# Turning half of the normalised rows by transposing transfers, in a kernel of two attention and two state-space layers

## The chip, the cores and the metric

The kernel runs on one core of one Trainium2 chip. The metric is the device time of one execution in microseconds, the median over several runs. A core has TensorE (matmuls, PE in the profile; its weight loads are PEld), ScalarE (ACT), VectorE (DVE), GpSimd (POOL), SyncE (SP, which here only issues transfers) and 16 DMA engines that serve the transfers of all queues. SBUF is the working memory of 128 partitions, PSUM the accumulators that TensorE writes.

## The reference

Four layers over a sequence of 2048 rows of 640 channels; each adds to its input what it computes from the normalised input. Layers 1 and 3 are attention with 32 heads of 20 channels, layers 2 and 4 a state-space convolution over the whole sequence (through an FFT):

```python
def _layernorm(x, axis=-1, eps=1e-5):
    m = jnp.mean(x, axis=axis, keepdims=True)
    v = jnp.var(x, axis=axis, keepdims=True)
    return (x - m) / jnp.sqrt(v + eps)

qkv = (x @ wqkv).reshape(B, S, 3, H, Dh).transpose(2, 0, 3, 1, 4)
p = softmax(einsum("bhqd,bhkd->bhqk", q, k) * Dh ** -0.5)
o = einsum("bhqk,bhkd->bhqd", p, v).transpose(0, 2, 1, 3).reshape(B, S, D) @ wo

K = 2.0 * einsum("dn,dnl->dl", C, exp(A * dt * pos)).real     # the filter of the convolution
y = irfft(rfft(u_t, 2 * L) * rfft(K, 2 * L))[:, :, :L] + u * D_skip

x = x + attention(layernorm(x)); x = x + s4d(layernorm(x))
x = x + attention(layernorm(x)); x = x + s4d(layernorm(x))
```

## The kernel before

The kernel is one program for a tile framework: the Python code issues instructions in an order, and a scheduler then places them on each engine. It goes by the order written as a priority and lets an instruction go first whose inputs are there earlier. On the chip every engine, and every engine's queue of transfers, then works through its own list strictly in order.

`attention` (from line 432) runs twice, once for layer 1 (`first_layer`) and once for layer 3. It has two parts. The long second part computes scores, exponentials and values wave by wave; ScalarE's exponentials fill it. This document is about the short first part (from line 756), the front, which makes what the first waves need:

- The 2048 rows are taken as 16 tiles of 128 rows, in four sets of four (`i4` = 0 to 3). In the first layer `load_x` loads a set from memory, into two buffers for each of the four tiles, so that one set can be loaded while another is worked on. In the later layer the rows lie in SBUF already.
- `ln_stats` gives mean and 1/deviation of each row (VectorE, with one square root on ScalarE). ScalarE then writes the normalised rows, f32, four activations of 128 x 640 a set (in the trace `xr<-xr,nb,rs` in the first layer and `xn<-x,nb,rs` in the later one).
- The projections need the rows turned, channels on the partitions. TensorE turns them in 128 x 128 blocks (line 823, tile `pst`): for each of five groups of channels (`ct`) four transposes fill one PSUM tile of 128 x 512. Each value is held as a sum of two f16 parts: ScalarE casts the PSUM tile into `xh` and VectorE writes the difference into `xl`. `xh` and `xl` are 128 x 5 x 2048 and hold all turned rows.
- `block0(i4)` (line 767) projects the set onto the first 128 columns of q and of k: for each 15 matmuls of 512 columns, five channel groups by three products of parts (`pq`, line 773). ScalarE copies the result (`qc`), and `post` (line 510) squares it, splits it into f16 parts `qhi` and `qlo` (two buffers each) and sends them to memory (`qs`, `ks`) by the SP queue.
- `values4(i4)` (line 779) computes v for the four tiles, 15 matmuls each (`pv`, line 586): 480 columns in the first layer, 160 in the later one. VectorE and ScalarE copy the result into `V`.
- The loop runs stats, normalisation, turning, `block0(i4)` and then `values4(i4 - 1)`, so the values lag a set behind. After the loop follow the norms of q and k (`norms`, `nrm`), their maximum (`longest`), the shift that goes to memory and comes back (`shift`, `qm`, `qop`), the first loads of `kop` and `qop`, and `values4(3)`.
- The scores' PSUM tiles are made from the space that the front's four `S` and two `M` tiles leave.

In the first layer a generator (`kgen`, line 198) makes powers for the convolution's filter beside all this: VectorE reduces angles, ScalarE takes exponentials and sines (`ke_`, `ks_`, `kc_`), SP stores them to memory (`wd`). The scheduler weaves its instructions into the front.

The two selectors that `norms` needs are loaded as f32 into a tile of their own (`self_`) and copied to `sel` at the first set.

Of the kernel before, what the change touches and what calls it, by code (L numbers as in the profile page):

```python
# [21 lines left out]
P = 128  # L22
L = 2048
D = 640
NI = L // P
NCT = D // P
H = 32
# [7 lines left out]
NBLK = len(BLOCKS)  # L35
# [11 lines left out]
QW = DH * 8  # L47
# [40 lines left out]
def mha_s4d_kernel(ctx, tc, x_in, wqkv, wo, lar, aim, cr, ci, ldt, dsk,  # L88
# [12 lines left out]
    se, ve, ge, sy = (Ordered(e, plan, tie, e is nc.vector) for e in (nc.scalar, nc.vector, nc.gpsimd, nc.sync))  # L101
# [330 lines left out]
    def attention(x, stats):  # L432
# [50 lines left out]
        def stage(c0, n, tag, dst=None, pool=None):  # L483

            full = QW if pool or tag == "v" else P
            ts = tag + "s" if pool else "ws"
            wt = (pool or q2).tile([P, NCT, QW], F32, tag=ts, bufs=1, name=ts)[:, :, :n]
            cols = c0 if isinstance(c0, tuple) else (c0,)
            m = n // len(cols)
            for k, c_ in enumerate(cols):  # L490
                sy.dma_start(wt[:, :, k * m:k * m + m], wqkv[:, c_:c_ + m].rearrange("(t p) c -> p t c", p=P))

            def make():
                bufs = 1 if tag == "v" else 2
# [12 lines left out]
            return make  # L507
# [249 lines left out]
        with ExitStack() as c2:  # L757
            psum(c2, M=2, S=4)
            hp = c2.enter_context(tc.tile_pool(name="hp", bufs=1))
            xp = c2.enter_context(tc.tile_pool(name="xnp", bufs=2))  # L760
            self_ = hp.tile([P, NBLK * H], F32, name="self")
            NQ = 3 if first_layer else 1
            wv = [hp.tile([P, NCT, NQ * QW], F16, name=f"wv{n}") for n in range(2)]
            wb = [[hp.tile([P, NCT, P], F16, name=f"wb{w_}{n}") for n in range(2)] for w_ in range(2)]
# [14 lines left out]
            def values4(i4):  # L779
                for i in range(4 * i4, 4 * i4 + 4):  # L780
                    for _ in values_of(i, 0, pst("M", [P, 512], F32, tag="mm", name="pv"), wv, NQ * QW):
                        pass

            def load_x(i4):

                if x is not None:
                    return [x[:, 4 * i4 + i, :] for i in range(4)]
                ts = [xp.tile([P, D], F32, tag=f"xr{i}", name=f"xr{i}") for i in range(4)]
                for i, t in enumerate(ts):
                    sy.dma_start(t, xv[:, 4 * i4 + i, :])  # L790
                return ts
# [4 lines left out]
                filler[:2] = kgen(), False  # L796
                weave(1)
            sy.dma_start(self_, c_sel)
            for i4 in range(4):
                xr = coming  # L800
                if i4 < 3:
                    coming = load_x(i4 + 1)
                if stats is None:
                    mv, rs = ln_stats(lambda i: xr[i], 4)
                else:
                    mv, rs = stats(i4)
                xn = []
                nb = sm.tile([P, 4], F32, tag="nb", name="nb")
                ve.scalar_tensor_tensor(nb, mv[:, :, 0], -1.0, rs, ALU.mult, ALU.mult)
                for i in range(4):  # L810
                    t = xr[i] if x is None else xp.tile([P, D], F32, tag=f"xr{i}", name=f"xn{i}")
                    se.activation(t, xr[i], AF.Identity, scale=rs[:, i:i + 1], bias=nb[:, i:i + 1])
                    xn.append(t)
                if i4 == 0:
                    for make in made_:
                        make()
                    made_ = [stage(2 * D + q * QW, QW, f"b{q}", [w[:, :, q * QW:q * QW + QW] for w in wv], hp)
                             for q in range(NQ)]
                    ve.tensor_copy(sel, self_)
                for ct in range(NCT):  # L820
                    pt = pst("S", [P, 512], F32, tag="S", name="pst")
                    for i in range(4):
                        te.transpose(pt[:, i * P:i * P + P], xn[i][:, ct * P:ct * P + P], ident)
# [3 lines left out]
                block0(i4)  # L827
                if i4 == 0:
                    for make in made_:
                        make()  # L830
                    nxt.append(stage((P, D + P), 64, "w"))
                else:
                    values4(i4 - 1)
# [960 lines left out]
```

## Time and profile before

| | |
|---|---|
| median of 3 runs | 2646.85 us (2645.38 to 2647.79) |
| profiled execution: span from first to last instruction | 2647.0 us |
| front of the first layer, first transpose to first scores | 17.5 to 115.8 us of the span |
| front of the later layer, first transpose to first scores | 1404.9 to 1468.6 us |
| granted TensorE clock, mean | 0.994 |

The profiled execution's own time is its span; it differs from the median of the runs by 0.15 us, so times taken from its trace can be set against the median as they stand. Times inside the trace are microseconds from the start of the span. Line 78 is a helper through which most instructions of VectorE, ScalarE, POOL and SP are issued, so these are told apart by their tiles, not by their line. TensorE's matmuls are pipelined: the start of the next one, not the length of one, says how much of the engine it took.

### The profile page before, as it was taken

How to read it: one execution, taken by the hardware profiler on the slowest of the kernel's cores; microseconds unless marked ns; L12 is line 12 of the kernel's file. 1: busy time of each engine (PE TensorE's matmuls, PEld its weight loads, DVE VectorE, ACT ScalarE, POOL GpSimd, SP SyncE). 2: the span in 40 equal slices, each digit the busy share in tenths (PEclk: the TensorE clock that was granted, in tenths of full speed). 3: DMA queues.
4: the chain of work that ended last, by engine and by line, in shares of the span. 5: the costliest groups of instructions: out<-in, count | busy, mean ns of one | idle time of the engine just before them, and what ended most of it. 6: DMA issues, size and time to landing. Idle time of an engine off the chain costs nothing.

```text
span 2647.0 us, 118800 instructions
## 1 busy us (share of the span) xinstructions
PE 2492.4 (94%) x52388; PEld 1409.8 (53%) x52388; DVE 1519.5 (57%) x3430; ACT 2344.0 (89%) x2763; POOL 801.7 (30%) x1230
## 2 busy tenths in 40 slices
PE   6899999999999999899898999999999998999898
PEld 3444444454444444587896544454444443444898
DVE  7587777777765887577786323232232222143875
ACT  7899999999999999655665899999999999999574
POOL 1123333233323332111681122222222223222285
PEclk9999999999999999999999999999999999999999
DMA  6522222322222221654652111121121113222466
GB/s 206 189 53 77 68 74 62 82 65 63 61 54 59 53 63 38 234 206 163 213 173 64 47 53 50 51 60 45 45 66 39 50 34 87 71 66 61 137 190 184
DMA packets 188158, 241.99 MB, mean 91 GB/s; under 512 B 43504, under 2 KB 128816, under 8 KB 186224
## 3 DMA queue, kind: packets, MB, share of 16 engines
q1 hardware_dynamic: 151936, 188.28, 22.6%
q0 software_dynamic: 35696, 46.01, 7.4%
q8 instruction: 413, 6.77, 1.1%
q14 instruction: 113, 0.93, 0.1%
HBM read 158.16 MB, written 76.00 MB: 88 GB/s over the span
## 4 chain that ended last, share of the span: by engine, by line
ACT 59%; PE 20%; issue 10%; DVE 3%; DMA 2%; POOL 1%; SPq 0%; ACTq 0%; POOLq 0%; DVEq 0%
ACT pt L78 57%; PE psy L1430 3%; PE pa L903 2%; PE psv L1430 2%; PE po L193 2%; PE psx L1430 2%; PE S L868 2%; PE pst L1452 1%; PE pkx L193 1%; PE pv L586 1%; PE m L620 1%; PE pkt L196 1%; PE pq L773 1%; DMA kb<-khb 1%; DMA kop<-ks 1%
## 5 line engine op out<-in xcount | busy, mean ns | idle before, releaser
L78 ACT ACTIVATE pt<-S 128x1024 f32<-128x1024 f32 x2048 | 1927.7, 1033 | 27.9 <-PE S L868 15.5
L903 PE MATMUL pa<-pt,V 64*32 64x512 f32 x16384 | 1096.9, 589 | 1.4 <-DVE oc L78 1.4
L868 PE MATMUL S<-qop,kop 61*32 61x512 f16 x16384 | 877.2, 380 | 82.7 <-ACT pt L78 67.8
L868 PEld LDWEIGHTS <-kop 61*32 61x32 f16 x16384 | 366.9, 89 | 737.3 <-issue 619.2
L903 PEld LDWEIGHTS pa<-pt,V 64*32 64x32 f32 x16384 | 312.7, 106 | 72.0 <-issue 8.6
L78 POOL DMA_DIRECT2D dn<-oc x248 | 122.7, 501 | 574.2 <-DVE oc L78 574.1
L78 DVE TENSOR_SCALAR qc<-m 128x512 f32<-128x512 f32 (+1 forms) x68 | 46.8, 688 | 312.0 <-PE m L620 312.0
L78 POOL DMA_DIRECT2D db<-dn x248 | 125.4, 512 | 141.5 <-DMA dn<-dr 136.9
L78 POOL DMA_DIRECT2D ot<-oc x256 | 130.5, 517 | 88.4 <-DVE oc L78 55.5
L620 PE MATMUL m<-xl,wh 64*32 64x512 f16 x2560 | 143.8, 376 | 0.3 <-issue 0.3
L620 PE MATMUL m<-xh,wh 64*32 64x512 f16 x2560 | 144.1, 378 | 0.0
L620 PE MATMUL m<-xh,wl 64*32 64x512 f16 x2560 | 143.8, 377 | 0.0
L78 DVE COPY oc<-pa 128x512 f32<-128x512 f32 x64 | 44.2, 690 | 172.9 <-PE pa L903 168.9
L78 ACT COPY xt<-pst 128x1024 f16<-128x1024 f16 x80 | 81.3, 1016 | 60.8 <-PE pst L1452 60.8
L620 PEld LDWEIGHTS <-wh 64*32 64x32 f16 x5120 | 90.3, 93 | 73.3 <-issue 30.8
L78 POOL DMA_DIRECT2D dn<-dr x62 | 34.6, 558 | 287.3 <-DVE dr L78 248.6
L1480 POOL TENSOR_TENSOR kb<-t,kb 128x512 f32<-128x512 f32 x76 | 97.2, 1280 | 65.2 <-DVE t L78 40.8
L78 DVE TENSOR_SCALAR V<-m 128x160 f32<-128x160 f32 x64 | 20.7, 324 | 163.4 <-PE m L586 163.4
L78 DVE TENSOR_TENSOR kb<-ktab 128x512 f32<-128x512 f32 x160 | 106.2, 683 | 0.0
L586 PEld LDWEIGHTS <-xh 128*128 128x128 f16 x960 | 79.7, 98 | 46.7 <-issue 31.4
L1480 POOL TENSOR_TENSOR ka<-ka,kb 128x512 f32<-128x512 f32 x76 | 97.5, 1283 | 6.0
L337 PEld LDWEIGHTS m<-kb,ka 128*32 128x32 f32 x3840 | 60.8, 109 | 71.0 <-issue 52.4
(312 smaller groups left out, 3936.4 us busy)
## 6 DMA issues: line engine op xcount, KB each, us to landing
ka<-kha SPq DMA_DIRECT2D x80, 256.0 KB
kb<-khb SPq DMA_DIRECT2D x80, 256.0 KB
db<-dn POOLq DMA_DIRECT2D x248, 64.0 KB, 3.2
kop<-ks SPq DMA_DIRECT2D x176, 80.0 KB
kpw<-wd POOLq DMA_DIRECT2D x60, 192.0 KB, 3.9
qop<-qs SPq DMA_DIRECT2D x256, 40.0 KB
ot<-oc POOLq DMA_DIRECT2D x256, 40.0 KB, 3.0
kha<-kn SPq DMA_DIRECT2D x20, 512.0 KB
```

The costliest lines, as they stand in the source:

```text
L78: made = f(out, *a, **k)
L193: chain(te.matmul(*a, **k))
L196: chain(te.transpose(*a, **k))
L337: chain(te.matmul(ps[32 * j:32 * j + 32, c8, :], a[n][:, ch, :], b[n][:, dd, :], start=(n == 0), stop=(n == 2), tile_position=(0, 32 * j)))
L586: chain(te.matmul(ps[:, :n], a_[:, ct, sl], m[:, ct, :], start=(k == 0), stop=(k == 14)))
L620: chain(te.matmul(ps[r][32 * t:32 * t + 32, :], a_[rows, ct, 32 * u:32 * u + 32], m[rows, ct, 512 * v:512 * v + 512], start=(k == 0), stop ...
L773: te.matmul(pq, a_[:, ct, :], m[:, ct, sl], start=(n == 0), stop=(n == 14))
L868: chain(te.matmul(S[32 * t:32 * t + 32, 512 * r:512 * r + 512], kt_[rows, kc + 32 * t:kc + 32 * t + 32], qt[rows, :], start=True, stop=Tru ...
L903: chain(te.matmul(pa[r][32 * j:32 * j + 32, :], V[rows, kt, VP * h:VP * h + 32], pts[j // 2][rows, 512 * (j % 2):512 * (j % 2) + 512], sta ...
L1430: at("pe", te.matmul(*a, **k))
L1452: at("pe", te.transpose(pt[:, k, g, :], of_group(x1[k], 4 * q + g), id16))
L1480: at("pool", getattr(ge, f)(*a))
```

## The change

The first two sets stay as they are. For sets 2 and 3, of each of four tiles:

- ScalarE writes the normalised rows straight as f16 (`nh`); VectorE computes them again in f32 (`t`); POOL subtracts and writes the rest as f16 (`nl`). `nh` and `nl` have two buffers each.
- Two transposing transfers on SP's queue turn `nh` into `xh` and `nl` into `xl`, each 128 x 640 to 5 blocks of 128 x 128. TensorE, PSUM and the copies out of PSUM have no part in it.

The code before the projections becomes a function `prepare`, the transposes by TensorE a function `turned`, and the order is written out: `prepare(2)` comes ahead of `block0(1)` and `values4(0)`, and `prepare(3)` ahead of `block0(2)` and `values4(1)`. The load of a set's rows, its statistics and its transfers stand in `prepare`. The selectors' f32 tile is dropped: they are loaded into the last columns of `xl`, which set 3 fills later.

```diff
-            self_ = hp.tile([P, NBLK * H], F32, name="self")
+            self_ = xl[:, NCT - 1, L - 2 * NBLK * H:].bitcast(F32)
...
-            for i4 in range(4):
-                xr = coming
+            def prepare(i4):
+
+                xr = coming.pop()
                 if i4 < 3:
-                    coming = load_x(i4 + 1)
+                    coming.append(load_x(i4 + 1))
...
                 for i in range(4):
+                    if i4 < 2:
+                        t = xr[i] if x is None else xp.tile([P, D], F32, tag=f"xr{i}", name=f"xn{i}")
+                        se.activation(t, xr[i], AF.Identity, scale=rs[:, i:i + 1], bias=nb[:, i:i + 1])
+                        xn.append(t)
+                        continue
+                    nh, nl = (xp.tile([P, D], F16, name=f"n{t}") for t in "hl")
+                    se.activation(nh, xr[i], AF.Identity, scale=rs[:, i:i + 1], bias=nb[:, i:i + 1])
                     t = xr[i] if x is None else xp.tile([P, D], F32, tag=f"xr{i}", name=f"xn{i}")
-                    se.activation(t, xr[i], AF.Identity, scale=rs[:, i:i + 1], bias=nb[:, i:i + 1])
-                    xn.append(t)
...
+                    ve.tensor_scalar(t, xr[i], mv[:, i, 0:1], rs[:, i:i + 1], ALU.subtract, ALU.mult)
+                    ge.tensor_sub(nl, t, nh)
+                    for a_, b_ in ((xh, nh), (xl, nl)):
+                        sy.dma_start_transpose(a_[:, :, 512 * i4 + i * P:512 * i4 + i * P + P], b_)
+                return xn
+
+            def turned(i4, xn):
...
+            coming = [coming]
+            xn = prepare(0)
...
+            turned(0, xn)
+            block0(0)
+            for make in made_:
+                make()
+            nxt.append(stage((P, D + P), 64, "w"))
+            turned(1, prepare(1))
+            prepare(2)
+            block0(1)
+            values4(0)
+            prepare(3)
+            block0(2)
+            values4(1)
+            block0(3)
+            values4(2)
```

More of the change, by code (lines that the diff above doesn't have):

```diff
@@ L810, in attention @@
                 for i in range(4):
-                    t = xr[i] if x is None else xp.tile([P, D], F32, tag=f"xr{i}", name=f"xn{i}")
-                    se.activation(t, xr[i], AF.Identity, scale=rs[:, i:i + 1], bias=nb[:, i:i + 1])
-                    xn.append(t)
[L814 to L819, printed above, removed]
+                    if i4 < 2:
[5 more added lines that the diff above has]
+                    se.activation(nh, xr[i], AF.Identity, scale=rs[:, i:i + 1], bias=nb[:, i:i + 1])
+                    t = xr[i] if x is None else xp.tile([P, D], F32, tag=f"xr{i}", name=f"xn{i}")
+                    ve.tensor_scalar(t, xr[i], mv[:, i, 0:1], rs[:, i:i + 1], ALU.subtract, ALU.mult)
[4 more added lines that the diff above has]
+            def turned(i4, xn):
                 for ct in range(NCT):
@@ L826, in attention @@
                     ve.tensor_sub(xl[:, ct, sl], pt, xh[:, ct, sl])
[L827 to L833, printed above, removed]
+            coming = [coming]
+            xn = prepare(0)
+            for make in made_:
+                make()
+            made_ = [stage(2 * D + q * QW, QW, f"b{q}", [w[:, :, q * QW:q * QW + QW] for w in wv], hp)
+                     for q in range(NQ)]
+            ve.tensor_copy(sel, self_)
+            turned(0, xn)
+            block0(0)
+            for make in made_:
+                make()
+            nxt.append(stage((P, D + P), 64, "w"))
[8 more added lines that the diff above has]
+            values4(2)
             for w_ in range(2):
```

## The prediction

> **What bounds the kernel now.** I read the page first: the span, the busy shares, the DMA queues.
>
> ```profile
> span 2647.0 us, 118800 instructions
> PE 2492.4 (94%) x52388; PEld 1409.8 (53%) x52388; DVE 1519.5 (57%) x3430; ACT 2344.0 (89%) x2763; POOL 801.7 (30%) x1230
> ...
> q1 hardware_dynamic: 151936, 188.28, 22.6%
> q0 software_dynamic: 35696, 46.01, 7.4%
> ```
>
> The change touches only the two stretches in front of the attentions, some 100 us and 65 us. So I cut those into windows: columns are length, busy time of PE, PEld, DVE, ACT, POOL, granted clock, DMA share, GB/s.
>
> ```profile
> 39.00:56.00 17.00, 14.64 (x81) 8.00 (x80) 14.71 (x41) 14.42 (x26) 0.00 (x0) 1.00 0.58 186
> 56.00:79.00 23.00, 21.25 (x111) 10.83 (x110) 14.30 (x32) 21.13 (x34) 0.00 (x0) 1.00 0.58 200
> 1424.00:1436.00 12.00, 11.79 (x96) 7.95 (x94) 6.52 (x13) 9.94 (x16) 0.00 (x0) 1.00 0.25 85
> 1436.00:1451.00 15.00, 14.96 (x124) 10.43 (x123) 8.79 (x18) 6.49 (x12) 0.00 (x0) 1.00 0.21 69
> ```
>
> In the second layer TensorE is simply full (14.96 of 15.00) and POOL and the DMA rings are nearly idle. In the first layer TensorE and ScalarE are both close to full, since the filter generator's sines share ScalarE, and the rings are already 58% busy. The chain of waits then says what ends each stretch. For the second layer:
>
> ```profile
> 1436.94 6.47 PE pq L773 x30
> 1443.42 3.94 PE pv L586 x57
> 1447.36 1.75 PE pst L823 x16
> ...
> 1449.99 6.48 PE pq L773 x30
> 1456.47 3.96 PE pv L586 x57
> ...
> 1466.96 1.35 DMA qop<-qm
> ...
> 1468.55 0.69 PE S L868 x8
> ```
>
> The transposes (pst) stand on that chain, between the block-0 projections (pq) and the values (pv), and the first scores follow by a fixed tail of norms and a round trip of the shift. Microseconds taken off TensorE before 1456 should come off the end. For the first layer the chain reaches back only to the last values, held by ScalarE and a transfer, so there it does not prove that TensorE bounds the earlier part:
>
> ```profile
> 97.73 1.96 DMA kop<-ks
> 99.69 0.62 ACT ks__1184 L78
> ...
> 100.84 14.01 PE pv L586 x60
> ```
>
> **What is removed.** Per layer, sets 2 and 3 lose 40 TensorE transposes, 10 ScalarE casts into xh and 10 VectorE subtractions into xl. TensorE's timeline around them (start, length, what):
>
> ```profile
> 50.92 1.91 PE L823 MATMUL pst<-ident,xr 128*128 128x128 f32 x16
> 53.67 0.36 PE L586 MATMUL pv<-wv,xh 128*128 128x480 f16 x1 [0.84 <-DVE V L78]
> 55.44 0.66 PE L823 MATMUL pst<-ident,xr 128*128 128x128 f32 x4 [1.41 <-DVE xl L78]
> ...
> 56.34 0.37 PE L586 MATMUL pv<-wv,xh 128*128 128x480 f16 x1
> 56.54 0.38 PE L773 MATMUL pq<-xh,wb 128*128 128x512 f16 x1
> ...
> 75.23 1.91 PE L823 MATMUL pst<-ident,xr 128*128 128x128 f32 x16
> ...
> 79.49 0.38 PE L773 MATMUL pq<-xh,wb 128*128 128x512 f16 x1
> ...
> 1434.14 1.91 PE L823 MATMUL pst<-ident,xn 128*128 128x128 f32 x16
> ...
> 1436.78 0.38 PE L773 MATMUL pq<-xh,wb 128*128 128x512 f16 x1
> ...
> 1447.20 1.91 PE L823 MATMUL pst<-ident,xn 128*128 128x128 f32 x16
> ...
> 1449.83 0.38 PE L773 MATMUL pq<-xh,wb 128*128 128x512 f16 x1
> ```
>
> First layer, set 2: from 50.92 to 56.54 is 5.62 us, in which four value matmuls also run, 0.20 apart (56.34 to 56.54), so 4.8 belong to the transposes and their waits; set 3: 75.23 to 79.49 is 4.26, less four again, 3.5. Second layer: 2.64 and 2.63, less three short value matmuls each (57 take 3.94, so 0.07 apiece), 2.4 and 2.4. All of it is 13.1 us; more TensorE time than that does not go.
>
> **What is added or moved.**
>
> ```profile
> L78 ACT CAST xh<-pst 128x512 f16<-128x512 f32 x40 | 21.1, 599 | 5.8 <-PE pst L823 5.8
> L78 DVE TENSOR_TENSOR xl<-pst,xh 128x512 f16<-128x512 f32 x40 | 25.0, 683 | 1.9 <-ACT xh L78 1.7
> L1236 POOL TENSOR_TENSOR ul<-u,uh 128x640 f16<-128x640 f32 x15 | 21.0, 1410 | 133.5 <-ACT uh L78 133.5
> 35.26 0.49 DVE L78 TENSOR_SCALAR kc__1081<-k_aim 128x640 f32<-128x640 f32 x1
> 1420.49 0.92 ACT L78 ACTIVATE xn<-x,nb,rs 128x640 f32<-128x640 f32 x1 [1.99 <-DVE nb L78]
> 39.66 2.50 SPq L78 DMA_DIRECT2D xr<-in_x_in  x4
> 45.43 0.32 SPq L78 DMA_DIRECT2D qs<-qhi  x1
> db<-dn POOLq DMA_DIRECT2D x248, 64.0 KB, 3.2
> kpw<-wd POOLq DMA_DIRECT2D x60, 192.0 KB, 3.9
> ```
>
> ScalarE: the normalisation now writes nh instead of xn, one for one (0.92 each), so ten casts of 0.60 less: 6.0 us of work off a layer. VectorE: ten subtractions of 0.68 (6.8 us) go and eight tensor_scalars over 640 columns come, 0.49 each by the nearest row, 3.9 us; a small relief. POOL: eight subtractions of exactly the form of the row at 1.41 us, 11.3 us a layer, on an engine that shows 0.00 busy in all four windows: no cost by themselves, but a link in the new chain. The statistics, the square root and the scale of sets 2 and 3 move ahead of a block; the scheduler already runs them that early (the first layer's first normalised row of set 2 appears below at 43.98, while block 1 computes), so I cost the move at nothing, hidden under pq of block 1. The selector's load only changes its place: the last columns of xl are written by set 3's transfers, long after sel is copied. Nothing.
>
> SP: sixteen transposing transfers a layer, each 160 KB (128 x 640 f16), each waiting for ScalarE or POOL, in one ordered queue. Behind a waiting one stand the qs and ks stores of the blocks and the first qop and kop loads; for the stores wait the two buffers of qhi and qlo, and so ScalarE's and VectorE's next splits. The loads are needed only at the end of the stretch.
>
> The trace before has no transposing transfer. Its pace, call it p per transfer, is the unknown, and bounds come from rows. Lower end: a 128 KB store takes the queue 0.32 us, and 160 KB in 128 whole rows at q1's mean packet (22.6% of 16 x 2647 us over 151936, 63 ns) take 0.50 us of the rings. Upper end: the rows arrive cut into 128-column blocks, so 640 pieces; at q0's mean packet of 88 ns over 16 engines, 3.5 us. Smaller pieces would cost more still, and no row excludes that. In between, the buffers set a pace of their own: nh and nl have two each; an nl buffer is held for 1.41 us on POOL and then until its transfer lands, 3.2 to 3.9 by the POOL queue's rows, say 3.5, together 4.9, so a row every 2.45 us and p = 1.23. The nearest row for the queue itself is the x load, 0.63 us each with twice the bytes, below that. I take p = 1.25, and keep 0.5 and 3.5 as ends.
>
> **When the sets land.**
>
> ```profile
> 43.98 0.91 ACT L78 ACTIVATE xr<-xr,nb,rs 128x640 f32<-128x640 f32 x1
> ```
>
> Second layer: the first half is ready at 1420.49 + 0.92 = 1421.4. Set 2 has landed 8p + about 3 later: 1434.4 (the landing's tail past the queue is about 3 of the 3.2 to 3.9). TensorE asks at 1434.14. Set 3 has landed at 1421.4 + 20 + 3 = 1444.4; TensorE, 4.8 us ahead, asks at 1445.0. Both just in time: the layer gains 4.8. Full gain holds to p = 1.29, and from p = 1.59 set 3 is no earlier than now (1449.83).
>
> First layer: the first half is ready at 44.9, set 2 lands at 57.9, TensorE would ask at 51.7 and got its transposes done at 56.54: a loss of 1.4 if TensorE waits, a gain up to 4.8 if the values of set 1 are put ahead of block 2 or the rows come earlier. I take 0. Set 3 (landed by 44.9 + 20 + 3 = 67.9) is well ahead of 75, so its 3.5 come off, provided that ScalarE's sines let the value copies through; the 6.0 us taken off ScalarE speak for that.
>
> **Sum.** 0 + 3.5 + 2.4 + 2.4 = 8.3 us. The profiled span is 2647.0, the median of the runs 2646.85, so nothing lies around it to add: 2647.0 - 8.3 = 2638.7, against the median 2638.6, say 2639.
>
> **A rule of the skill against the change.** TensorE's 16 transposes of 128 x 128 take 1.91 us, 0.12 each, and the cost on the other side is p. The Trainium skill, VectorE: DVE Perf Modes, section The three transpose paths, gives 1309 ns for a 128 x 128 block by the DMA crossbar against 390 ns by TensorE, and its rules advise TensorE where PSUM will do. As an estimate from that page, five blocks in series would be 6.5 us a transfer, and by it the time would be some 2800 us (rival (a) with p = 6.5). DMA: Bandwidth & Descriptors, section Latency and other measured facts, has 261 GB/s for such transfers, 0.63 us for 160 KB as an estimate, and with it the buffers would set the pace. No run here shows either yet.
>
> **Rivals.**
> (a) The transfers are slow: p of 2.2 or more. This one ends slower. Place: set 3's last transfer, for which block 3's matmuls wait with all of TensorE behind them. At p = 2.5 the second layer's set 3 lands at 1421.4 + 40 + 3 = 1464.4, 14.6 after 1449.83; the first layer's at 87.9, 8.4 after 79.49: 23 us, 2670. At p = 3.5 it is 31 + 24, 2702. The page's rule above speaks for this rival. It decides from p = 1.6 on in the second layer and from (79.49 - 44.9 - 3)/16 = 1.97 in the first. For it: full TensorE, and no row of such a transfer. Against: rings at 21 to 25% in the second layer.
> (b) Hidden but not worth anything: p between 1.5 and 1.9. The second layer breaks even or loses up to 5, the first keeps its 3.5: 2647, give or take 4.
> (c) The first layer's end is held by the generator, not by TensorE. For it: the chain there runs through ScalarE's ks and a transfer, and ScalarE is 21.13 of 23.00 busy. Then only the second layer gains: 2647.0 - 4.8 = 2642.2.
>
> **Chances.** 0.2% of the median is 5.3 us, about what a measurement tells from no change. Forecast (2639, its own range 2632 to 2642): 0.42. Rival (c) 0.16, mostly within 0.2% and a quarter beyond. Rival (b) 0.14, within. Rival (a) 0.28, slower. So faster 0.45, same 0.26, slower 0.29. The range runs from 2632 (all 13.1 off is 2633.9, and a little for ScalarE's relief) to 2670, which leaves out p above 2.5 (0.16) and some 0.03 below.
>
> **What would show it.** Right: no pst on TensorE after set 1; pq of blocks 2 and 3 follow values with under 1 us between; the second layer's first scores at 1468.55 less 4.8 and less the first layer's 3.5, near 1460; a transposing transfer of 1 us or less on SP. Wrong: TensorE waiting for a transfer into xh or xl in front of pq, a granted clock under 1.00 after it; ScalarE's qhi waiting for stores held behind transfers; in the first layer the last values waiting for ScalarE as long as TensorE was early.

## The result, and the profile after

The changed kernel takes 2663.28 us (median; 2661.41 to 2668.04) against 2646.42 (2644.36 to 2647.79) on the same chip: a ratio of 1.0068, 95% interval 1.0055 to 1.008. It is 17 us slower; 8 us faster had been forecast. The profiled execution of after has a span of 2661.5 us, 14.5 more than before. The other 2.4 us are before's: in its 80 other executions the time is 1.7 to 1.9 us longer than the span, so the profiled one, with a span of 2647.0, took an estimated 2648.8, 2.4 above the median. "Nothing lies around it to add" was therefore a misreading, and every row of before comes from an execution slower than the median. In after's listing the transposes are line 831, the transposing transfers 823, POOL's subtraction 821 and the scores 890.

The page of after:

```profile
span 2661.5 us, 118715 instructions
...
q1 hardware_dynamic: 173440, 193.53, 23.8%
```

SP's queue carries 21504 packets more, 672 for each of the 32 transfers. The windows, with the same columns as before (the later layer's are moved by the 6 us by which it starts later):

```profile
39.00:56.00 17.00, 12.37 (x52) 5.06 (x51) 14.98 (x37) 12.09 (x18) 6.36 (x4) 0.86 0.95 225
56.00:79.00 23.00, 20.32 (x93) 9.18 (x92) 11.56 (x19) 13.09 (x20) 6.35 (x4) 0.96 0.64 127
1430.00:1442.00 12.00, 10.00 (x76) 6.11 (x74) 11.35 (x18) 6.80 (x12) 4.84 (x4) 1.00 0.68 120
1442.00:1457.00 15.00, 11.83 (x86) 7.81 (x86) 7.12 (x11) 6.04 (x9) 5.90 (x4) 0.89 0.61 132
```

TensorE has less to do and is no longer full. The DMA engines' rings (the share column) went from 0.25 and 0.21 to 0.68 and 0.61 in the later layer and from 0.58 twice to 0.95 and 0.64 in the first. VectorE is nearly full where the new rows are written (11.35 of 12 us, 6.52 before). ScalarE has gone from 21.13 to 13.09 busy in 56 to 79, more than the casts that it lost (10 of 0.60 us in the whole layer): it waits.

TensorE's timeline in the later layer, first two rows of before, then after (start, length; idle before and its releaser in brackets):

```profile
1404.92 0.66 PE L823 MATMUL pst<-ident,xn 128*128 128x128 f32 x4 [1.14 <-DVE st L78]
...
1460.34 0.89 PE L548 MATMUL nrm<-sq,sel 128*32 128x512 bf16 x8
```

```profile
1444.29 0.43 PE L586 MATMUL pv<-wv,xh 128*128 128x160 f16 x2 [3.10 <-DVE V L78]
...
1458.38 0.38 PE L773 MATMUL pq<-xh,wb 128*128 128x512 f16 x1
1461.94 0.59 PE L773 MATMUL pq<-xl,wb 128*128 128x512 f16 x1 [3.18 <-DMA kop<-ks]
...
1471.01 0.30 PE L586 MATMUL pv<-wv,xh 128*128 128x160 f16 x2
...
1475.26 0.88 PE L548 MATMUL nrm<-sq,sel 128*32 128x512 bf16 x8
...
1483.14 1.19 PE L890 MATMUL S<-qop,kop 61*32 61x512 f16 x16 [2.16 <-DMA qop<-qm]
```

Counted from the layer's first transpose (pst, 1404.92 before, 1411.26 after), block 3 starts 2.2 us late (47.1 against 44.9), takes 12.6 us instead of 6.5 because set 3's last xl lands only in front of its second matmul (the wait is put down to kop, the transfer next to it on the queue), and the norms (nrm) come 8.6 us late (64.0 against 55.4). ScalarE's first two rows of set 2 and SP's queue show why the last transfer was late:

```profile
1427.63 0.92 ACT L78 ACTIVATE nh<-x,nb,rs 128x640 f16<-128x640 f32 x1 [2.00 <-DVE nb L78]
...
1432.80 1.74 ACT L78 ACTIVATE nh<-x,nb,rs 128x640 f16<-128x640 f32 x2
```

```profile
1428.58 1.24 SPq L823 DMA_TRANSPOSE xh<-nh  x1
1430.45 1.20 SPq L823 DMA_TRANSPOSE xl<-nl  x1
1431.70 0.70 SPq L78 DMA_DIRECT2D qop<-qs  x1
...
1434.08 1.02 SPq L78 DMA_DIRECT2D qop<-qs  x2
1435.20 1.36 SPq L823 DMA_TRANSPOSE xh<-nh  x1
...
1440.57 1.68 SPq L78 DMA_DIRECT2D qop<-qs  x3
...
1457.43 1.70 SPq L823 DMA_TRANSPOSE xl<-nl  x1
```

The pace is what had been taken (1.23 us in the median of the 16). But from the first transfer to the end of the last it is 30.6 us and not 20: 20.1 for the 16 transfers, 7.2 for loads and stores among them, 3.2 idle.

In the first layer much of the loss comes by another road. ScalarE's, SP's and VectorE's timelines:

```profile
61.88 0.83 ACT L78 ACTIVATE kc__1068<-kc__1068,hpi 128x640 f32<-128x640 f32 x1
...
62.57 1.39 SPq L823 DMA_TRANSPOSE xh<-nh  x1
64.06 3.40 SPq L823 DMA_TRANSPOSE xl<-nl  x2
...
74.71 1.23 SPq L823 DMA_TRANSPOSE xl<-nl  x1
...
77.09 0.45 SPq L78 DMA_DIRECT2D wd<-kc__1068  x1
...
79.41 0.49 DVE L78 TENSOR_SCALAR kc__1094<-k_aim 128x640 f32<-128x640 f32 x1 [4.94 <-DMA wd<-kc__1068]
...
81.85 0.74 ACT L78 ACTIVATE ks__1093<-ks__1093 128x640 f32<-128x640 f32 x1 [7.74 <-DVE kc__1094 L78]
...
121.05 0.81 ACT L78 ACTIVATE kc__1198<-kc__1198,hpi 128x640 f32<-128x640 f32 x1
...
123.18 2.85 ACT L78 ACTIVATE pt<-S 128x1024 f32<-128x1024 f32 x3
```

The generator's power kc__1068 was finished at 62.7, its store went out 14.4 us later, behind seven transposing transfers, and until it had landed VectorE could not refill the buffer. ScalarE then had nothing to do for 7.7 us. Counted in the timeline, the generator had started 10 of its activations on ScalarE by 80 us instead of 14, and its last one started at 121.05 instead of 112.69. The first exponential (pt) follows it at 123.18. In the kernel before it did not:

```profile
112.69 0.83 ACT L78 ACTIVATE kc__1221<-kc__1221,hpi 128x640 f32<-128x640 f32 x1
...
117.80 2.85 ACT L78 ACTIVATE pt<-S 128x1024 f32<-128x1024 f32 x3
```

There 4.3 us lay between, and the exponential waited for the scores (115.78). So the generator is not the whole loss: counted from the first transpose (17.50 before, 15.22 after) the first exponential comes 7.7 us later, 4.3 of them because the first scores do (102.6 against 98.3 us), and 3.4 because the exponential then stands 5.4 us behind the scores instead of 2.0. TensorE too waited for landings in this layer, 3.71 and 0.92 us in front of block 2.

### The profile page after: what moved, and what is told of

Same layout as the page of the kernel before. It is cut to its first block, busy times and chain, and to the rows that moved or that the text cites. A ratio compares the mean times of both kernels' runs of the same rounds, so it can differ in the third digit from the quotient of the medians.

```text
span 2661.5 us, 118715 instructions
## 1 busy us (share of the span) xinstructions
PE 2491.9 (94%) x52308; PEld 1401.3 (53%) x52308; DVE 1525.7 (57%) x3426; ACT 2335.0 (88%) x2743; POOL 825.4 (31%) x1246
## 4 chain that ended last, share of the span: by engine, by line
ACT 57%; PE 21%; issue 13%; DVE 5%; DMA 3%; POOL 1%; SPq 0%; ACTq 0%; POOLq 0%; DVEq 0%
ACT pt L78 54%; PE pa L925 4%; PE psy L1452 2%; PE S L890 2%; PE po L193 2%; PE psv L1452 2%; PE psx L1452 2%; PE m L620 1%; PE pst L1474 1%; PE pkx L193 1%; PE pkt L196 1%; DVE x L78 1%; PE pkf L193 1%; DMA kop<-ks 1%; POOL kb L1502 0%
## 5 line engine op out<-in xcount | busy, mean ns | idle before, releaser
L78 ACT ACTIVATE pt<-S 128x1024 f32<-128x1024 f32 x2048 | 1927.8, 1033 | 30.3 <-PE S L890 15.9
L620 PEld LDWEIGHTS <-wh 64*32 64x32 f16 x5120 | 89.8, 93 | 73.0 <-issue 30.6
```

The source lines that it names most:

```text
L78: made = f(out, *a, **k)
L620: chain(te.matmul(ps[r][32 * t:32 * t + 32, :], a_[rows, ct, 32 * u:32 * u + 32], m[rows, ct, 512 * v:512 * v + 512], start=(k == 0), stop ...
```

## The experiments

All runs but nh_twice (below) beside each other. "First" is the first layer's front from its first transpose to the first exponential, "later" the later layer's from first transpose to first scores, both from the one profiled execution, which can lie some us off the median. The ratio is to the kernel before on the same chip (medians of 2644.8 to 2646.7 us). In the three runs with a star the first exponential says too little: the generator was not finished there and went on to 125.5 to 128.9 us, with the other exponentials behind it.

| run | median us | ratio, 95% | first | later |
|---|---|---|---|---|
| before | 2646.42 | | 100.30 | 63.63 |
| after | 2663.28 | 1.0068 (1.0055 to 1.008) | 107.96 | 71.88 |
| order_alone | 2649.13 | 1.0016 (1.0008 to 1.0025) | 98.96 | 65.03 |
| first_only | 2662.10 | 1.0065 (1.0052 to 1.0078) | 108.72 | 64.05 |
| later_only | 2653.91 | 1.0045 (1.003 to 1.006) | 97.92 | 69.69 |
| later_bufs4 | 2661.57 | 1.0068 (1.0056 to 1.008) | 107.62 | 69.02 |
| nl_dve | 2666.97 | 1.0082 (1.0067 to 1.0097) | 108.58 | 70.09 |
| wd_pool | 2666.09 | 1.0081 (1.0067 to 1.0095) | 111.90 | 67.98 |
| all_pool * | 2662.71 | 1.0068 (1.0054 to 1.0081) | 104.84 | 71.44 |
| xl_act | 2693.11 | 1.0183 (1.0169 to 1.0197) | 116.28 | 91.05 |
| dead_transfers | 2665.76 | 1.0074 (1.0062 to 1.0086) | 111.14 | 70.35 |
| dead_stores_pool * | 2666.24 | 1.0072 (1.0059 to 1.0085) | 107.98 | 68.51 |
| stores_pool_dve * | 2670.64 | 1.0097 (1.0083 to 1.0112) | 107.42 | 71.60 |
| hi_and_nl | 2654.66 | 1.0027 (1.0017 to 1.0036) | 104.05 | 67.38 |
| hi_only | 2648.65 | 1.0006 (0.9997 to 1.0015) | 100.32 | 62.12 |
| nl_zero | 2645.58 | 0.9997 (0.9988 to 1.0005) | 99.21 | 61.19 |
| last_set | 2653.44 | 1.0026 (1.0017 to 1.0035) | 104.55 | 63.78 |
| later_two | 2652.95 | 1.0030 (1.0019 to 1.0041) | 98.17 | 69.49 |
| later_two_dve | 2654.92 | 1.0030 (1.0018 to 1.0042) | 98.98 | 68.59 |

### Order and layers apart

order_alone keeps the order and turns all sets by TensorE:

```diff
-                    if i4 < 2:
+                    if i4 < 4:
...
-            prepare(2)
+            xn = prepare(2)
             block0(1)
             values4(0)
+            turned(2, xn)
```

> The new order and the selectors' new place are kept, but all four sets are turned by TensorE (no transposing transfer, no second f32 row on VectorE, no work on POOL). The change cost 17 us (2663.3 against 2646.4). Theory 1 (the loss is in the turning, that is in the chain ScalarE, POOL, transfer): 2646 within 3 us, the later layer's front about 63.6 us long as before. Rival, theory 2 (the order itself costs, because the statistics and activations of the next set are put ahead of the copies that a block waits for on ScalarE): 2652 or more, with ScalarE's qc waiting or late in both fronts.

The order costs about 4 us by the medians. Its two fronts, 1.3 shorter and 1.4 longer, do not show where: its profiled execution has the same span as before's (2646.9 and 2647.0), which was 2.4 above the median. first_only makes the change in the first layer alone, later_only (with `not first_layer`) in the later one:

```diff
-                    if i4 < 2:
+                    if i4 < 2 or not (first_layer):
...
+            if first_layer:
                 turned(1, prepare(1))
...
+            else:
+                for i4 in range(1, 4):
+                    turned(i4, prepare(i4))
+                    block0(i4)
+                    values4(i4 - 1)
```

> Only the first layer is changed; the later one has the order and TensorE's transposes of before. In the changed kernel's trace the first exponentials of the first layer start 5.4 us later than before (123.18 against 117.80) and that shift is 6.4 at the later layer's first transpose. If the two layers' losses are independent: about 2646.4 + 6.4 = 2653. If the loss in the later layer is caused by what the first leaves behind (a different placement of buffers), it would show here as well: above 2658.

> Only the later layer is changed. Independent losses: 2646.4 + 8.2 = about 2655, with the front from first transpose to first scores some 71.8 us long (63.6 before, 71.8 with the whole change). If the later layer's loss hangs on the first one's: within 3 us of before.

Each layer loses by itself, the first 9 us more than expected. By its time first_only came out on the side of the rival (above 2658), but not by the rival's mechanism: its later front is as before (64.05). The two ratios add up to 1.011, not to 1.0068; why stays open.

### One cure at a time

later_bufs4 takes nh and nl from the xn buffers that sets 2 and 3 leave free:

```diff
-                    nh, nl = (xp.tile([P, D], F16, name=f"n{t}") for t in "hl")
...
+                        n2 = xp.tile([P, 2, D], F16, tag=f"xr{2 + i % 2}", name="n2")
+                        nh, nl = n2[:, 0, :], n2[:, 1, :]
```

> The whole change, but in the later layer nh and nl have four buffers each instead of two (they share space with buffers of normalised rows that sets 2 and 3 do not need). Theory A (two buffers: ScalarE, in order, stands before nh until a transfer that takes 3 us has landed, and the casts of the blocks stand behind it): the later layer's waits of nh for a transfer fall from 9 us to under 2, block 3's matmuls start some 8 us earlier and the time is 2655 or a little less. Theory B (SP's one queue, with 16 transfers of 1.23 us among loads of qop and kop and stores, sets the rate): rows come no sooner, 2661 to 2664. Theory C (VectorE and POOL slow each other while both work on whole rows): VectorE's splits still take 1.5 us instead of 0.7, and of the 8 us at most 3 come back.

The front gains 2.9 us on after instead of the 8 expected, and the time none that can be measured. ScalarE's waits for a buffer fell only from 9.0 to 5.1 us, because nh and nl now share a buffer that is held until nl's transfer has landed. So four buffers are no cure; that the buffers have no part is not shown.

nl_dve moves the subtraction:

```diff
-                    ge.tensor_sub(nl, t, nh)
+                    ve.tensor_sub(nl, t, nh)
```

> The whole change; the subtraction for nl is done by VectorE instead of POOL, so that POOL has no work in the fronts. Theory C (VectorE and POOL slow each other: while POOL subtracts, VectorE's sq and qlo take 1.5 to 1.9 us instead of 0.69, and its rows 1.1 to 1.5 instead of 0.55, and TensorE then waits 3 us for VectorE's copies of V): sq, qlo and the rows are back at 0.69 and 0.55, the waits of 3 us for V in the later layer go, and of the 17 us some 4 to 6 come back, 2658. Rival: the 8 subtractions cost VectorE 0.85 us each, 6.8 us a layer, as much as the slowing did, and rows come no sooner since two buffers and SP's queue hold them: 2661 to 2666.

VectorE's squares between 1426 and 1460, by shape (count, busy, mean ns), first in after, then in nl_dve:

```profile
L78 DVE TENSOR_TENSOR sq<-qc 128x512 bf16<-128x512 f32 x5 | 5.9, 1176 | 5.3 <-ACT qc L78 5.3
```

```profile
L78 DVE TENSOR_TENSOR sq<-qc 128x512 bf16<-128x512 f32 x5 | 3.4, 687 | 5.7 <-ACT qc L78 5.7
```

The slowing by POOL is real (1176 against 687 ns in the mean for the same instruction; three of the five in after were slowed, up to 1.89 us). But VectorE now does the subtractions itself, 8 of 0.82 us, and no time comes back.

wd_pool sends the generator's stores by POOL's queue, all_pool also the q and k stores of block 0 and the first kop and qop loads; xl_act issues nl's transfers from ScalarE:

```diff
-            sy.dma_start(wd[:, 2, n, :], e)
+            ge.dma_start(wd[:, 2, n, :], e)
...
-                        sy.dma_start((ks if u else qs)[...], ...)
+                        (ge if pool else sy).dma_start((ks if u else qs)[...], ...)
...
-                load_k(0, j, 0)
-                load_q(0, j, 0, 0)
+                load_k(0, j, 0, ge)
+                load_q(0, j, 0, 0, ge)
...
-                        sy.dma_start_transpose(a_[...], b_)
+                        (sy if a_ is xh else nc.scalar).dma_start_transpose(a_[...], b_)
```

> The whole change; only the generator's stores of its powers (wd) go from SP's queue to POOL's. Theory G (first layer: these stores stand in SP's one queue behind transposing transfers that wait for rows; VectorE waited 4.9 us for the store of kc__1068, which was issued only at 77.09, and ScalarE was idle for 7.7 us; what was left of the generator's work then pushed the value copies and the first exponentials back): the first layer's front gives back most of its 8.6 us (4.3 before the first scores, 4.3 between first and second scores), about 2655, and ScalarE's idle of 7.7 us is gone. Rival, theory L (the first layer loses by TensorE's waits for landings, 3.71 and 0.92 us in front of block 2, and by the slow clock after them): no better than 2660.

> The whole change; the generator's stores, the stores of q and k of the fronts' block 0 and the first loads of kop and qop all go by POOL's queue, so SP keeps the transfers of rows, weights and the 32 transposing ones. Theory B (SP's queue sets the rate: in the later layer 16 transfers of 1.23 us and 5.3 us of others filled 25 of 27.4 us between the first transposing transfer and the last): the later layer's last transposing transfer is issued some 5 us earlier relative to the layer's first transpose, block 3 starts that much earlier, and with the first layer's 8.6 us of theory G the time is 2650. Theory A or C alone (buffers, VectorE beside POOL): the later layer's front stays at 69 to 72 us, so 2655 at best. Against both: POOL's own issues could be slow and come between its subtractions.

> The whole change; the transposing transfers of nl go by ScalarE's queue, those of nh stay on SP's, so each queue has 8 of 16 a layer. Theory B (SP's queue): the last rows land some 5 us earlier in the later layer, 2658 or less. Rival (the chain through ScalarE, POOL and two buffers sets the rate; and now ScalarE, in order, waits for POOL before it can issue, with the casts of the blocks behind): 2663 or more, with the later layer's nh rows no closer together.

None helps. In wd_pool the generator is on time at 80 us (14 activations) and late again afterwards: POOL, in order too, stands before nl's buffers with the stores behind it (up to 5.8 us for a landing), so the wait had only been moved. In all_pool the norms of the later layer come 4.9 us earlier than in after (59.1 against 64.0), so the queue does hold that layer back; a new wait of 6.8 us for qop<-qm, which stands on POOL's queue here, takes it away again. In its first layer nothing is gained, though the first exponential comes earlier. ScalarE's timeline:

```profile
121.73 1.02 ACT L78 ACTIVATE pt<-S 128x1024 f32<-128x1024 f32 x1
...
124.71 0.81 ACT L78 ACTIVATE kc__1198<-kc__1198,hpi 128x640 f32<-128x640 f32 x1
...
126.84 2.85 ACT L78 ACTIVATE pt<-S 128x1024 f32<-128x1024 f32 x3
```

One exponential comes through before the generator ends; the others follow 3.7 us later than in after. In xl_act ScalarE itself stands at its queue; its timeline:

```profile
1449.34 6.61 ACTq L823 DMA_TRANSPOSE xl<-nl  x2
1456.04 0.60 ACT L78 ACTIVATE qc<-pq 128x512 f32<-128x512 f32 x1 [11.19 <-issue]
```

For 11 us the copy of a finished block waits behind two transfers, and TensorE waits up to 14.8 us for V. That run shows nothing about the load of SP's queue.

### Transfers that nobody waits for

dead_transfers is order_alone with the 16 transfers beside it, into two scratch buffers:

```diff
                         xn.append(t)
+                        if i4 > 1:
+                            for a_ in (xh, xl):
+                                z = xp.tile([P, NCT, P], F16, name="z")
+                                sy.dma_start_transpose(z, a_[:, i, 384 * (i4 - 2):384 * (i4 - 2) + D])
```

> The new order with all four sets turned by TensorE, and beside it the 16 transposing transfers a layer at the same places of the program, from parts of xh and xl into two small buffers that nobody reads. So SP's queue and the rings carry what the change put on them, but no engine waits for the result. The order alone gave 2649. Theory R (the transfers themselves do the harm: rings at 70 to 96% and an occupied SP queue hold up the generator's stores, the loads and the stores of q and k): 2656 or more, with the first layer's generator late as with the change. Rival, theory D (the harm is that work waits for what the transfers deliver: rows, the chain through ScalarE and POOL, two buffers): within 3 us of the order alone, 2646 to 2652.

This is the sharpest of the runs: the transfers alone cost as much as the whole change, 12.2 us in the first front and 5.3 in the later one over order_alone (9.0 and 6.9 for the change). No engine needs what they deliver; only SP's queue itself stood 2.4 us before the two scratch buffers. Its SP and ScalarE timelines:

```profile
60.13 0.58 SPq L78 DMA_DIRECT2D wd<-kc__1112  x1
...
76.52 0.45 SPq L78 DMA_DIRECT2D wd<-kc__1122  x1
...
1465.76 1.25 SPq L819 DMA_TRANSPOSE z<-xl  x1
1467.05 0.58 SPq L78 DMA_DIRECT2D qs<-qhi  x1
...
1469.81 0.62 ACT L78 CAST qhi<-qc 128x512 f16<-128x512 f32 x1 [5.19 <-DMA qs<-qhi]
```

No store of the generator for 16.4 us; and in the later layer a store of q behind transfers, for which ScalarE's next split waits 5.2 us, behind that VectorE's copy of V, and TensorE 3.8 us for V. dead_stores_pool adds POOL's queue for the stores of the generator and of block 0 (the first two edits of all_pool above); stores_pool_dve is the whole change with these two edits and that of nl_dve:

> As dead_transfers (all sets turned by TensorE, 16 transposing transfers a layer into buffers that nobody reads), with the generator's stores (wd) and block 0's stores of q and k on POOL's queue, where nothing else stands in the fronts. Theory Q (SP's queue: the stores stand behind transposing transfers; in dead_transfers no wd store was issued between 60.13 and 76.52, and ScalarE's qhi waited 5.19 us for a store of q): both losses go, 2649 as with the order alone, 18 of its generator's activations done by 80 us instead of 10. Rival, theory R (the rings: the same bytes in small packets fill them whatever queue the stores use): 2660 or more.

> The whole change, with the generator's stores and block 0's stores of q and k on POOL's queue and nl's subtraction on VectorE, so that POOL has nothing that waits for rows or buffers (which is what held up the stores when they were moved alone). Theory Q: the generator's share of the loss and ScalarE's waits for stores go; what stays is TensorE's waits for landings: 2653 to 2656. Rival (the chain of rows sets the time, not the stores): 2663 or more.

dead_stores_pool says both yes and no. In the later layer the norms are back at 56.3 us behind the first transpose (62.3 in dead_transfers, 56.4 in order_alone), so up to there the stores behind transfers were all of it; then a wait of 6.7 us for qop<-qm takes 4 back. In the first layer 3.2 of the 12.2 us seem to return, but the generator is not finished at the first exponential (124.74; its last activation starts at 127.72), and the later layer's first transpose comes 2.6 us later than in dead_transfers (1417.29 against 1414.70): nothing is left of them, and the time is the same. POOL's and VectorE's timelines and a window there, and behind them SP's and VectorE's of the kernel before:

```profile
71.68 0.54 POOL L78 DMA_DIRECT2D wd<-kc__1138  x1 [0.29 <-issue]
...
78.81 0.49 DVE L78 TENSOR_SCALAR kc__1164<-k_aim 128x640 f32<-128x640 f32 x1 [6.24 <-DMA wd<-kc__1138]
...
70.00:80.00 10.00, 8.41 (x50) 4.97 (x49) 3.72 (x10) 5.95 (x12) 3.64 (x7) 1.00 1.07 242
```

```profile
71.92 0.32 SPq L78 DMA_DIRECT2D wd<-kc__1107  x1
...
74.21 0.50 DVE L78 TENSOR_SCALAR kc__1133<-k_aim 128x640 f32<-128x640 f32 x1 [1.49 <-DMA wd<-kc__1107]
```

This store is issued in time and VectorE resumes 7.1 us later; in the kernel before, the store of kc__1107 left at 71.92 and VectorE went on at 74.21, 2.3 us later. The rings' share is 1.07 in these 10 us (0.54 before). POOL's queue by itself is not that slow: behind its stores at 63.95, 88.05 and 98.79 VectorE resumed within 2.7 to 3.2 us, at shares of 0.60 to 0.80. So in the first layer the full rings have a part of their own. How large it is stays open. stores_pool_dve came out with its rival (2663 or more), 7 us over after; why it is slower than after stays open.

### Half the transfers, and the link taken away

nh_twice was to leave out VectorE's second row and POOL's subtraction by transposing nh into xl as well:

> The whole change with 16 transposing transfers a layer, but both come from nh: VectorE's second f32 row and POOL's subtraction are left out (so xl holds the wrong part for sets 2 and 3), and a row waits for ScalarE alone. Theory C (VectorE's rows beside POOL's subtractions slow VectorE, whose copies of V TensorE waits for): the waits of 3 us for V in the later layer are gone and its front is 66 us or less instead of 71.9; 2655 in all. Rival (SP's queue, the rings and nh's two buffers set the rate): the last transposing transfer of the later layer is issued as late as with the change, 46 us behind the layer's first transpose, and the time is 2660 to 2664.

It took 28,586 us and tells nothing of the question: with nh in the place of the rest, the program left its fast form, and the matmuls of its general form of attention (`gS`, `gpo`) fill the trace. nl_zero takes the second transfer of a pair from a tile of zeros, `((xh, nh), (xl, nz))`, without VectorE's rows and POOL's subtractions. hi_and_nl is the changed kernel with the 8 transfers of nl a layer left out and xl set to zero by POOL beforehand, as in the diff (the selectors then go into the last columns of xh); hi_only is hi_and_nl without VectorE's rows and POOL's subtractions:

```diff
-                    for a_, b_ in ((xh, nh), (xl, nl)):
+                    for a_, b_ in ((xh, nh),):
...
+            ge.memset(xl[:, :, L // 2:], 0.0)
```

> The whole change with its 16 transposing transfers a layer, but the second of each pair comes from a tile of zeros: VectorE's second f32 row and POOL's subtraction are left out, and xl is zero for sets 2 and 3. Theory C (VectorE slowed by POOL and loaded with 8 more rows): the waits of 3 us for V in the later layer go, its front is 67 us instead of 71.9, 2657 or less. Theory Q (SP's queue, which has as many transfers as before): 2661 to 2665.

> The change with only the 8 transposing transfers of nh a layer: xl is zero for sets 2 and 3 and was set so beforehand, and VectorE's second row and POOL's subtraction are left out. Theory Q (8 transfers fewer free SP's queue for 10 us a layer): most of the loss goes and TensorE's shorter path shows, 2645 or less. If the rest of the loss has another cause (two buffers of nh, the order): 2650 or more.

> The change with VectorE's second f32 rows and POOL's subtractions in place, but nl is not transferred: xl was set to zero for sets 2 and 3 beforehand, and 8 transposing transfers a layer remain. If the number of transfers is the cause: as hi_only, 2646 to 2651. If the link (VectorE's rows, POOL beside VectorE) is: it stays at 2658 or more; 2652 to 2657 would mean that both have a share.

In nl_zero the zero tile was ready at once, and the scheduler put its transfers ahead of the crowded stretch; so it is, like hi_only, a run with 8 transfers there and no link. hi_and_nl then separates the two. From after to hi_and_nl the 8 transfers, with the waits for their landing, are worth 3.9 us in the first front and 4.5 in the later one; from there to hi_only the link through VectorE and POOL is worth 3.7 and 5.3 (in that step the selectors' place in memory differs too). hi_only stands 1.5 us under before in the later layer.

Both runs carry a cost of their own in the later layer, the zeroing of xl. POOL's and VectorE's timelines in hi_only:

```profile
1401.38 4.36 POOL L78 MEMSET xl<- 128x5120 f16 x1 [3.04 <-ACT lt L78]
...
1402.50 3.26 DVE L78 TENSOR_SCALAR lt<-lt 128x4 f32<-128x4 f32 x1
```

The same VectorE instruction takes 0.15 us in nl_zero, before and after; here it ends with POOL's memset. Set 0's last transposes then start 8.6 us behind the first in both runs, 6.5 in after and 6.6 in before. So in that layer the transfers are worth an estimated 6.6 us instead of 4.5, and hi_only would stand 3.6 under before instead of 1.5.

The times give another split. Over the kernel before on the same chip the medians are 16.9 us (after), 7.9 (hi_and_nl) and 2.3 (hi_only): 8.9 for the transfers, 5.7 for the link, and no gain left. hi_only's profiled execution was 1.7 us under its median and hi_and_nl's 0.8 over, which explains part of the difference. TensorE's timeline in nl_zero shows the intended effect:

```profile
1433.39 0.38 PE L775 MATMUL pq<-xh,wb 128*128 128x512 f16 x1
...
1444.01 0.38 PE L775 MATMUL pq<-xh,wb 128*128 128x512 f16 x1
...
1462.43 0.83 PE L889 MATMUL S<-qop,kop 61*32 61x512 f16 x8 [1.90 <-DMA qop<-qm]
```

Blocks 2 and 3 start at 32.2 and 42.8 us behind the first transpose (31.9 and 44.9 before), and the front is 2.4 us shorter. In the time this does not show (a ratio of 0.9997, and the profiled execution was 3.5 us under the median).

### Candidates

later_two is later_only with the four buffers and set 3 prepared a block sooner; later_two_dve also has nl on VectorE. last_set turns only set 3 by transfers, in both layers:

```diff
                 prepare(2)
+                prepare(3)
                 block0(1)
                 values4(0)
-                prepare(3)
...
-                    if i4 < 2:
+                    if i4 < 3:
```

> A candidate: only the later layer is changed, with four buffers for nh and nl, and both sets 2 and 3 are prepared right behind set 1, ahead of block 1. Theory T (the rows start too late: set 2's second row is written only 4 us behind its first, because ScalarE turns set 1 between, and set 3's rows stand behind block 1's casts): the 16 transfers take 16 x 1.23 = 20 us plus 5 us of other transfers from about 17 us behind the first transpose, so the last is issued at 42, lands at 45, block 3 starts on time (44.9 before, less 2.4 saved): the front is 62 us against 63.6, 2645. Rival (VectorE beside POOL, and SP's queue, still hold block 2 and the values back): 66 us or more, 2649 to 2653.

> As the candidate before, with nl's subtraction on VectorE, so that POOL does not slow VectorE. If the contention of VectorE and POOL is what is left once buffers and order are mended: no wait of TensorE for V over 1 us, front 61 to 62 us, 2644. If VectorE itself is then too full in front of block 2 (8 more subtractions, 0.85 us each): block 2 is 2 to 4 us late, 2648 to 2651.

> A candidate with a complete result: only set 3 is turned by transposing transfers, in both layers (8 a layer, VectorE's rows and POOL's subtractions for that set), set 2 by TensorE. If the loss grows with the number of transfers out of proportion, because SP's queue and the rings have room for 8 and not for 16: 2644 to 2650. If it is in proportion: 8 to 9 us, 2655.

None beats the kernel before. Rows asked for earlier change nothing (69.49 against 69.69 in later_only), since in front of block 2 TensorE still waits 3.8 us for V. last_set loses 6.7 us by the medians, two fifths of what the whole change does, and nearly all of it in the first layer.

## Why the prediction was wrong

- **Bound: right; saving: too large.** The transposes stood on the path in the later layer, and taking them off is worth 2.4 us in nl_zero's later front, half of the 4.8 forecast, because block 2 still waits 2.1 us for V. No run shows a gain in the time, nor the 3.5 us forecast for the first layer.
- **The pace p: right.** 1.23 us against 1.25 taken. Rival (a) had the right side and almost the right time (2670), and the right place in the later layer, block 3 waiting for the last transfer; but its condition, p of 2.2 or more, was not met: that its time comes close is luck. By the 1309 ns a block of the Trainium skill (VectorE: DVE Perf Modes, The three transpose paths) in series it would have been an estimated 6.5 us a transfer; the trace has 1.23 for five blocks.
- **"When the sets land": wrong.** It let 16 transfers follow one another at p from the first row on. Rows and queue had other work: the second row was written 5.2 us behind the first (1432.80 against 1427.63), and 7.2 us of other transfers lay among the 16. Set 3 was forecast 39.5 us behind the first transpose, and TensorE resumed at 50.7.
- **SP's queue: named, and priced at nothing.** The text said that the stores stand behind the transfers and that ScalarE's and VectorE's splits wait for them; no term of the sum followed. The generator's wd stores, on the same queue, were missed altogether. Beside them the rings, 58% busy in the first layer, were taken as free. The transfers of nl alone, half of the load, measured 8.4 us in the two fronts with the waits for their landing (some 10.5 without the zeroing of xl, 8.9 by the medians).
- **"A small relief" on VectorE and "no cost by themselves" on POOL: wrong.** Together, with the waits for V behind them, 9.0 us by the fronts and 5.7 by the medians. VectorE's busy time did not go down but up, from 1519.5 to 1525.7 us in the whole execution. The new rows also come in front of the copies of V that TensorE needs, and they and the squares get slower while POOL works. The Trainium skill, SBUF — State Buffer, section Who interferes with whom, says that a VectorE instruction with two inputs in SBUF contends with a GpSimd instruction that reads SBUF, and that the later one blocks; the trace agrees, 1176 against 687 ns above.
- **Rival (c): half right, and its size wrong.** In the kernel before, the first layer's front ended with the scores, 4.3 us behind the generator. With the change the generator's last activation starts 8.4 us later (121.05 against 112.69) and then does hold the first exponential, which comes 5.4 later. The rival was priced as a lost gain only, not as a loss.

As steps from one run to the next, 8.4 and 9.0 less the 1.5 that hi_only gains make up the 7.7 + 8.2 = 15.9 us by which the two fronts are longer. That they add up is so by construction and tests nothing; and 2.3 of the 7.7 are an earlier first transpose in after's profiled execution. What is shown is that both steps cost several us, by fronts and by medians, and that transfers into unread buffers are enough for a loss of this size. The costs overlap: those transfers alone cost 17.5 us in the two fronts, where the whole change costs 15.9 over the same order_alone, link included.

What POOL's slowing and what VectorE's extra rows do in the second step stays open. So does the split of the first between queue and rings in the first layer, the part of the two buffers, and the 4 us of order_alone.

## What to carry to other kernels

Before giving an idle queue a row of transfers, list everything else that queue carries and who waits for each: a store behind a transfer holds its buffer, and the engine that wants the buffer may be far from the change. Price work moved to an engine with room by what it stands in front of there, not by the engine's total. And put the suspected load into the old kernel with nobody waiting for it: that one run showed that carrying the transfers is enough for the loss, without anyone waiting for them.

## What was not expected of the hardware

A pause of TensorE of more than 3 us can cost about twice its length. Windows of after in the first layer, around a pause of 3.71 us and one of 0.92 just behind it:

```profile
48.00:52.00 4.00, 0.37 (x2) 0.00 (x0) 3.59 (x7) 1.76 (x4) 2.32 (x2) 0.89 0.96 186
52.00:58.00 6.00, 5.00 (x12) 1.62 (x13) 4.52 (x17) 4.00 (x6) 0.00 (x0) 0.50 0.61 182
58.00:62.00 4.00, 4.00 (x20) 1.76 (x18) 3.06 (x7) 2.75 (x5) 0.42 (x1) 1.00 0.17 56
```

The granted clock is 0.50 for the 6 us from 52 to 58, and matmuls start every 0.43 us instead of 0.215. In the later layer's block 3 a pause of 3.18 us brought another 3.0 that way: the block took 12.6 us instead of 6.5. A pause of 1.96 us (at 70.21) left the clock at 1.00. The Trainium skill, TensorE: Matmul & The Clock Gate, section What's actually happening, has the clock fall to half after an idle window of about 3.4 us and rise after a busy one; the pauses of 3.1 to 3.7 us agree roughly; the 6 us of slow clock, with the second pause in them, are longer than one such window.
